# Clustered attention with a gated layer on one core: softmax factors spread from a DRAM row, and the second head's operands and masks placed by the list planner

## The chip, the cores and the metric

The kernel runs on one core of a Trainium2 chip. The metric is the device time of one execution in microseconds (us). Before the change it is 609.67 us, the median of 3 runs (608.6 to 610.37). The core has a tensor engine for matrix products (PE, whose weight loads are shown apart as PEld), a vector engine (DVE), a scalar engine (ACT), a general engine (POOL), and a sync engine (SP) that here issues every DMA. Each engine works through its own instructions in the order in which they were written; semaphores hold an instruction until what it reads is ready.

## The reference

Attention for 32 heads (4 batches of 8), in which a query sees only the keys whose nearest centroid is the same as its own, and behind it a layer that multiplies a projection with a gate from a short convolution, and projects again.

```python
def _attn_ref(q, k, v, centroids):            # q, k, v (4, 8, 768, 64), centroids (8, 16, 64)
    ...
    q_assign = np.argmax(np.einsum('bhsd,hcd->bhsc', q_n, c_n), axis=-1)
    k_assign = np.argmax(np.einsum('bhsd,hcd->bhsc', k_n, c_n), axis=-1)
    mask = q_assign[:, :, :, None] == k_assign[:, :, None, :]
    scores = scale * np.matmul(q, k.transpose(0, 1, 3, 2))
    scores = np.where(mask, scores, -1000000000.0)
    scores = scores - np.max(scores, axis=-1, keepdims=True)
    attn = np.exp(scores)
    attn = attn / (np.sum(attn, axis=-1, keepdims=True) + 1e-09)
    return np.matmul(attn, v).astype(np.float32)

def _moe_ref(x, w_val, conv_w, w_out):        # x (4, 768, 512) is the attention's output, heads side by side
    ...
    for k in range(K):                        # K = 5 taps along the sequence
        gate_pre += conv_w[k][None, None, :] * xp[:, k:k + S, :]
    gate = 1.0 / (1.0 + np.exp(-gate_pre))
    val = x @ w_val
    return (gate * val @ w_out).astype(np.float32)
```

## The kernel before

**Tiling.** A head has 768 queries in 6 tiles of 128, so there are 192 tiles; a tile is called a slot, in the order in which the tiles are computed. Heads go in 16 pairs. The first 12 slots take the heads 0 and 1 in alternation: three tiles of head 0, three of head 1, then the other three of each. Per tile, `qk` forms 128 by 768 scores in PSUM as two sums of matmuls (L410 and L415): q and k are split into a rounded high part and a remainder, called x2 and x1 for q (`prep_x2`, `prep_x1`), y1 and y2 for k (`prep_y1`, `prep_y2`), and the cluster masks are extra rows written into the operands x2 and y2 (`prep_mask0` for the first pair, `prep_mask` by DMA for the others), so that the mask comes out of the same matmul. Then DVE takes the row maximum (`rowmax`, L422), ACT the exponential with its row sum (`expo`, L431), PE transposes the tile in two groups of three blocks (L486), ACT copies these out of PSUM (`evict`, L493), and PE multiplies with v (`av`, L504).

**Softmax factors.** A pair's half (3 tiles of each of 2 heads) ends with 6 row sums per query row. `recip` inverts them on DVE (L438, L439). They lie along the partitions, but the attention output is transposed, with channels on the partitions and queries along the row, so the factors have to be spread: `recip_row` copies the 768 numbers by two DMAs into one row of one SBUF partition (the tile rr, L457), and `recip_rows` reads that row 64 times per head into 128 partitions by two DMAs (the tile rs, L464). POOL then multiplies (`scale_x`, L523). This happens 30 times. The last pair uses PE for it (`recip_b`, `recip_t`, `recip_out`).

**What sets the order.** A planner at the end of the kernel's construction holds all work as operations (`Op`: kind, engine, assumed duration, predecessors, buffers, due slot `dl`), simulates the engines with assumed costs and writes the instructions in the order that it finds. An `Op` with two engines in its table may go to either if its kind is in `FLEX`. DMAs go by the table `DMA` (time on SP, time to landing). `SIZE` holds how many buffers a name has. The planned part starts from `free`, the times at which the engines are taken to be free at its start. Ahead of the planned part stands a start-up written out by hand at the end of the function: first loads, cluster indices of the first pair, the operands of head 0, and before the change also those of head 1, with all but three of the first pair's mask copies. 94 matmuls without use (`warm`) keep PE busy in it.

**What waits on SP.** SP issues DMAs strictly in order, about 0.5 us each, so a DMA whose source isn't ready holds every one behind it.

Of the kernel before, what the change touches and what calls it, by code (L numbers as in the profile page):

```python
# [8 lines left out]
F32 = mybir.dt.float32  # L9
# [4 lines left out]
AF = mybir.ActivationFunctionType  # L14
# [3 lines left out]
P = 128  # L18
# [7 lines left out]
def kernel(  # L26
# [314 lines left out]

    def prep_x1_first(h, c0, c1):

        if ops[h][0] is None:
            ops[h][0] = operand(h, 0)
        t = gate[:, 2 + h, c0:c1]
        G.tensor_scalar(t, raws["q", h][:, c0:c1], QS, 0.0, op0=ALU.mult, op1=ALU.add)
        G.tensor_tensor(ops[h][0][:, c0:c1], t, ops[h][1][:, c0:c1].bitcast(F32), op=ALU.subtract)
# [27 lines left out]
    def prep_mask0(h, i, hf):  # L376


        n = C * (h + 1)
        dst, r = ops[h][1 + 2 * i][D:D + n, hf * HALF:(hf + 1) * HALF], 64 * hf + 32 * i  # L380
        src = oh[r:r + n, 0:HALF]
        if i == 0 and h == 0:
            S.activation(dst, src, AF.Copy)
        elif i == 0:
            G.tensor_scalar(dst, src, 1.0, 0.0, op0=ALU.mult, op1=ALU.add)
        elif h == 0:
            V.tensor_scalar(dst, src, BIG, -BIG, op0=ALU.mult, op1=ALU.add)
        else:
            S.activation(dst, src, AF.Identity, bias=oh_b1[r:r + n], scale=oh_s1[r:r + n])
# [61 lines left out]
    def recip_row(p, hf):  # L451

        sm = sums[p, hf]
        rr = sums[p, hf] = ring(am_p, 1, [P, 2, HALF], F32, "rr")[0:1]
        with nc.allow_non_contiguous_dma(reason="768 elements"):
            for e in range(2):
                nc.sync.dma_start(out=rr[:, e].rearrange("o (q t) -> o q t", t=TPH), in_=sm[:, e])  # L457

    def recip_rows(p, hf):

        rr = sums[p, hf]
        rs = ring(am_p, 1, [P, HALF], F32, "rs")
        for e in range(2):
            nc.sync.dma_start(out=rs[e * D:(e + 1) * D], in_=rr[:, e].unsqueeze(1).broadcast_to([1, D, HALF]))  # L464
# [8 lines left out]

    def recip_out(p, hf):
        acc = sums[p, hf]
        rs = sums[p, hf] = ring(am_p, 1, [P, 2, HALF], F32, "rr")[:, 0]
        S.activation(rs, acc[:, 0:HALF], AF.Copy)

    tps = {}
# [60 lines left out]
    def sigm(t, c0, c1):  # L540
# [6 lines left out]
    BURST, MBURST = 4, 4  # L547
    TOL = {"V": 0.2, "A": 0.15, "G": 2.0}
    DECODE = [24, 29, 34, 39, 52, 57, 62, 67]
    T1X = 5.0  # L550


    FLEX = ("X2", "Y1", "W1", "W3")
    CLASH = 0.8


    DMA = {"LQ": (1.15, 4.5), "LK": (1.15, 4.5), "LS": (0.42, 4.8), "LV": (0.42, 4.8), "RR": (1.2, 3.2), "RS": (1.1, 8.0),
           "MK": (1.0, 4.2), "W0": (0.6, 8.5), "ST": (0.45, 3.5)}

    hs, macc = {}, {}  # L560
# [41 lines left out]
    def proj_store(b, ch, t):  # L602
# [113 lines left out]

# [56 lines left out]
    for p in range(NPAIR):  # L773
        for hf in range(2):
# [303 lines left out]
```

## Time and profile before

| | before |
|---|---|
| median of 3 runs | 609.67 us |
| the profiled execution | 609.94 us |
| its span, first to last instruction | 608.2 us |
| DVE busy | 429.7 us (71%) |
| ACT busy | 428.3 us (70%) |
| POOL busy | 286.3 us (47%) |
| granted PE clock, mean | 0.992 |
| HBM read and written | 48.29 and 6.29 MB |

The span is 1.7 us shorter than the profiled execution; the rest lies around it. Busy times are of instructions on the engine. Times inside the trace count from the span's start. In the view by stages a row has a stretch of the span, its length, then the busy time and the number of instructions of PE, PEld, DVE, ACT and POOL, then the granted PE clock (1.00 is full speed), the mean busy share of the 16 DMA engines and the rate that they moved. In a timeline a row has start, duration, engine, line, operation, what is written <- what is read, the number of instructions, and in brackets the idle time before it with what ended it.

### The profile page before, as it was taken

Reading aid. Unit: us, or ns where it says so; the run is one execution under the profiler, and the core shown is the slowest. Engines: PE = TensorE matmul, PEld = TensorE weight load, DVE = VectorE, ACT = ScalarE, POOL = GpSimd, SP = SyncE. Lnnn points to the kernel's source line nnn. Section 1 sums busy time; section 2 is a strip of 40 time slices with the busy share of each in tenths; the row PEclk is TensorE's granted clock in tenths of the full one; section 3 lists DMA queues with packets and bytes.
Section 4 is the critical chain, followed back from the end, with each engine's and each line's share of the span. In section 5 each row is a group of like instructions: output and inputs, shape, how many; then the busy total and the mean of one; then the engine's idle time right before and its main releaser. Section 6 shows DMA issues by size and latency. Waiting matters only on the chain.

```text
span 608.2 us, 10379 instructions
## 1 busy us (share of the span) xinstructions
PE 581.2 (96%) x3592; PEld 436.3 (72%) x3592; DVE 429.7 (71%) x591; ACT 428.3 (70%) x924; POOL 286.3 (47%) x302
## 2 busy tenths in 40 slices
PE   6788899999999998999999999999999999999997
PEld 5655656566878775777786777778687777877786
DVE  5896998889889574779685476965977656863420
ACT  4856968788767775787876767777787777786321
POOL 5531767256442465294641344613653325562521
PEclk9897999999999999999999999999999999999999
DMA  8677586876787646766665667655668676431011
GB/s 246 165 115 162 125 109 121 136 113 90 133 133 101 120 54 165 136 95 96 80 128 131 90 116 125 100 62 143 76 135 134 89 133 71 21 13 38 17 53 52
DMA packets 42197, 64.21 MB, mean 106 GB/s; under 512 B 14752, under 2 KB 26912, under 8 KB 42144
## 3 DMA queue, kind: packets, MB, share of 16 engines
q1 hardware_dynamic: 42144, 63.55, 61.6%
q8 instruction: 28, 0.46, 0.3%
q14 instruction: 25, 0.20, 0.1%
HBM read 48.29 MB, written 6.29 MB: 90 GB/s over the span
## 4 chain that ended last, share of the span: by engine, by line
PE 73%; DVE 8%; DMA 7%; SPq 4%; ACT 4%; issue 2%; POOL 2%; ACTq 0%; DVEq 0%; POOLq 0%
PE acc L504 17%; PE tp L486 17%; PE sp L410 9%; PE sp L415 8%; PE acc L569 7%; PE acc L594 6%; DMA sraw<-kT 3%; PE sp L594 3%; PE sp L569 3%; DVE gate L538 3%; DVE nm L422 3%; SPq L285 2%; PE acc L290 2%; ACT pr L431 2%; DMA raw<-kT 1%
## 5 line engine op out<-in xcount | busy, mean ns | idle before, releaser
L422 DVE TENSOR_REDUCE nm<-sp 128x1 f32<-128x768 f32 x192 | 181.6, 952 | 102.2 <-PE sp L415 92.2
L493 ACT ACTIVATE pt<-tp 128x384 f32<-128x384 f32 x384 | 175.8, 492 | 76.8 <-PE tp L486 75.9
L431 ACT ACTIVATE pr<-sp,nm 128x768 f32<-128x768 f32 x192 | 173.5, 904 | 36.0 <-DVE nm L422 29.2
L486 PEld LDWEIGHTS tp<-ident,pr 128*128 128x128 f32 x1152 | 133.8, 141 | 60.1 <-issue 18.7
L486 PE MATMUL tp<-ident,pr 128*128 128x128 f32 x1152 | 168.7, 278 | 8.5 <-ACT pt L493 5.9
L504 PE MATMUL acc<-pt,vt 128*64 128x384 f32 x768 | 136.6, 495 | 0.2 <-ACT pt L493 0.2
L410 PE MATMUL sp<-op,op 128*128 128x384 f32 x372 | 111.9, 382 | 5.7 <-ACT pr L431 5.2
L538 DVE SCALAR_TENSOR_TENSOR gate<-xr,cw,gate 128x768 f32<-128x768 f32 (+1 forms) x84 | 84.1, 1006 | 18.7 <-POOL gate L86 17.9
L415 PE MATMUL sp<-op,op 80*128 80x384 f32 (+1 forms) x372 | 96.3, 340 | 0.0
L504 PEld LDWEIGHTS acc<-pt,vt 128*64 128x64 f32 x768 | 50.4, 137 | 62.1 <-issue 59.1
L523 POOL TENSOR_TENSOR xr<-xr,rs 128x384 f32<-128x384 f32 x30 | 34.9, 1163 | 112.7 <-ACT xr L516 81.1
L362 POOL TENSOR_TENSOR op<-raw,op 128x384 fp32r<-128x384 f32 x62 | 72.2, 1181 | 11.6 <-ACT op L84 10.8
L415 PEld LDWEIGHTS sp<-op,op 80*128 80x128 f32 (+1 forms) x372 | 68.4, 191 | 0.0
L410 PEld LDWEIGHTS sp<-op,op 128*128 128x128 f32 x372 | 57.1, 193 | 11.1 <-ACT pr L431 8.6
L86 POOL TENSOR_SCALAR op<-raw,qsc 128x768 fp32r<-128x768 f32 x25 | 24.2, 969 | 83.6 <-PE sp L415 77.9
L585 POOL TENSOR_TENSOR h<-gate,h 128x384 fp32r<-128x384 f32 x32 | 35.5, 1117 | 40.5 <-ACT h L581 40.5
L594 PE MATMUL acc<-wh_o,h 128*128 128x512 f32 x144 | 48.9, 399 | 0.0
L340 DVE SCALAR_TENSOR_TENSOR op<-raw,op 128x768 fp32r<-128x768 f32 x30 | 38.7, 1291 | 0.3 <-POOL op L86 0.2
L431 ACT ACTIVATION_READ_ACCUMULATOR pr<-sp,nm 128x1 f32 x192 | 38.8, 202 | 0.0
L530 POOL TENSOR_TENSOR xl<-xr,xh 128x768 fp32r<-128x768 f32 (+1 forms) x21 | 33.1, 1579 | 0.6
L569 PE MATMUL acc<-xh,wh_v 128*128 128x384 f32 x96 | 33.3, 347 | 0.0
L569 PE MATMUL acc<-xh,wl_v 128*128 128x384 f32 x96 | 32.3, 337 | 0.0
(133 smaller groups left out, 635.9 us busy)
## 6 DMA issues: line engine op xcount, KB each, us to landing
raw<-qT SPq DMA_DIRECT2D x62, 192.0 KB, 3.3
raw<-kT SPq DMA_DIRECT2D x62, 192.0 KB, 5.4
sraw<-qT SPq DMA_DIRECT2D x32, 192.0 KB, 4.9
sraw<-kT SPq DMA_DIRECT2D x32, 192.0 KB, 5.1
vt<-v SPq DMA_DIRECT2D x16, 384.0 KB, 4.2
out_dram<-ob SPq DMA_DIRECT2D x24, 256.0 KB, 2.4
rs<-rr SPq DMA_DIRECT2D x60, 96.0 KB, 7.6
op<-oht SPq DMA_DIRECT2D x56, 48.0 KB, 4.6
```

Source lines behind the costliest of these rows:

```text
L340: V.scalar_tensor_tensor(x1[:, c0:c1], raws["q", h][:, c0:c1], QS, x2[:, c0:c1], op0=ALU.mult, op1=ALU.subtract)
L362: G.tensor_tensor(y2[:, c], raws["k", h][:, c], ops[h][2][:, c].bitcast(F32), op=ALU.subtract)
L410: PE.matmul(sp[:, hf, 0:HALF], x1[:, ts_], y1[:, hf * HALF:(hf + 1) * HALF], start=True, stop=False)
L415: PE.matmul(sp[:, hf, 0:HALF], x2[0:KR, ts_], y2[0:KR, hf * HALF:(hf + 1) * HALF], start=False, stop=True)
L422: V.tensor_reduce(out=nm, in_=sp[:, :, 0:HALF], op=ALU.max, axis=AX.XY, negate=True)
L431: S.activation(pr.rearrange("p (a b) -> p a b", a=2), sp[:, :, 0:HALF], AF.Exp, bias=nm, scale=1.0, accum_out=sums[h // 2, hf][:, h % 2, t ...
L486: PE.transpose(tp[:, i * P:(i + 1) * P], pr[:, j * P:(j + 1) * P], ident)
L493: S.activation(o, tps.pop((h, t, g))[:, 0:HALF].rearrange("p (a b) -> p a b", b=P), AF.Copy)
L504: PE.matmul(acc[e * D:(e + 1) * D, 0:HALF], vt[:, j, e * D:(e + 1) * D], pts[2 * p + e, hf][:, j, :], start=(j == 0), stop=(j == NT - 1),)
L538: V.scalar_tensor_tensor(g, xr[:, k + c0:k + c1], cw[:, ct, k:k + 1], g, op0=ALU.mult, op1=ALU.add)
L569: PE.matmul(macc[b, ch, m][:, 0:HALF], a[:, kt, ms], x[:, kt, cs], start=(kt == 0 and i == 0), stop=(kt == NC - 1 and i == 2))
L594: PE.matmul(macc[b, ch, t][:, 0:DM], x[:, kt, ts_], a[:, kt, :], start=(kt == 0 and i == 0), stop=(kt == NC - 1 and i == 2))
```

## The change

1. `recip_row` writes the 768 factors with one DMA into a tile rr in DRAM (2 rows of 384, two such tiles), in place of two DMAs into a row of one SBUF partition. `recip_rows` spreads them from there, again with two DMAs. The planner's costs follow: RR takes SP 0.7 instead of 1.2, RS lands after 4.8 instead of 8.0, rr has two buffers. `recip_out` of the last pair takes the tile rs instead of rr.
2. The operands of head 1 (x2, x1, y1, y2) and its two mask copies into x2 leave the hand-written start-up and become operations of the planner, as its two mask copies into y2 already were. x2 and y1 may go to POOL or ACT; x1 comes in two halves that may go to POOL (two instructions) or DVE (one); one mask copy of head 0 may go to POOL or ACT. Three mask copies of head 0 stay written out, two of them on ACT and one on DVE, where both copies of `prep_mask0(0, 1, ...)` were on DVE.
3. `free` and the assumed arrival of head 1's q and k (`T1Q`, `T1K`) are set anew. As the planner starts from other times and other costs, the order of nearly the whole list comes out different.

```diff
+    dr_p = ctx.enter_context(tc.tile_pool(name="dr_p", bufs=1, space=bass.MemoryType.DRAM))
...
     def prep_x1_first(h, c0, c1):
 
+        if on[0] == "V":
+            prep_x1(h, c0, c1)
+            return
         if ops[h][0] is None:
             ops[h][0] = operand(h, 0)
         t = gate[:, 2 + h, c0:c1]
...
         n = C * (h + 1)
         dst, r = ops[h][1 + 2 * i][D:D + n, hf * HALF:(hf + 1) * HALF], 64 * hf + 32 * i
         src = oh[r:r + n, 0:HALF]
-        if i == 0 and h == 0:
+        if i == 0 and on[0] == "A":
             S.activation(dst, src, AF.Copy)
         elif i == 0:
             G.tensor_scalar(dst, src, 1.0, 0.0, op0=ALU.mult, op1=ALU.add)
-        elif h == 0:
+        elif h == 0 and on[0] == "V":
             V.tensor_scalar(dst, src, BIG, -BIG, op0=ALU.mult, op1=ALU.add)
         else:
-            S.activation(dst, src, AF.Identity, bias=oh_b1[r:r + n], scale=oh_s1[r:r + n])
+            x, b = (oh_s, oh_b) if h == 0 else (oh_s1, oh_b1)
+            S.activation(dst, src, AF.Identity, bias=b[r:r + n], scale=x[r:r + n])
...
     def recip_row(p, hf):
 
         sm = sums[p, hf]
-        rr = sums[p, hf] = ring(am_p, 1, [P, 2, HALF], F32, "rr")[0:1]
+        rr = sums[p, hf] = ring(dr_p, 2, [2, HALF], F32, "rr")
         with nc.allow_non_contiguous_dma(reason="768 elements"):
-            for e in range(2):
-                nc.sync.dma_start(out=rr[:, e].rearrange("o (q t) -> o q t", t=TPH), in_=sm[:, e])
+            nc.sync.dma_start(out=rr.rearrange("e (q t) -> q e t", t=TPH), in_=sm)
...
     def recip_rows(p, hf):
 
         rr = sums[p, hf]
         rs = ring(am_p, 1, [P, HALF], F32, "rs")
         for e in range(2):
-            nc.sync.dma_start(out=rs[e * D:(e + 1) * D], in_=rr[:, e].unsqueeze(1).broadcast_to([1, D, HALF]))
+            nc.sync.dma_start(out=rs[e * D:(e + 1) * D], in_=rr[e:e + 1].broadcast_to([D, HALF]))
         sums[p, hf] = rs.rearrange("p (q t) -> p t q", t=TPH)
...
     def recip_out(p, hf):
         acc = sums[p, hf]
-        rs = sums[p, hf] = ring(am_p, 1, [P, 2, HALF], F32, "rr")[:, 0]
+        rs = sums[p, hf] = ring(am_p, 1, [P, HALF], F32, "rs")
         S.activation(rs, acc[:, 0:HALF], AF.Copy)
...
-    T1X = 5.0
-
-
-    FLEX = ("X2", "Y1", "W1", "W3")
+    T1Q, T1K = -1.7, -0.2
...
-    DMA = {"LQ": (1.15, 4.5), "LK": (1.15, 4.5), "LS": (0.42, 4.8), "LV": (0.42, 4.8), "RR": (1.2, 3.2), "RS": (1.1, 8.0),
+    DMA = {"LQ": (1.15, 4.5), "LK": (1.15, 4.5), "LS": (0.42, 4.8), "LV": (0.42, 4.8), "RR": (0.7, 3.2), "RS": (1.1, 4.8),
            "MK": (1.0, 4.2), "W0": (0.6, 8.5), "ST": (0.45, 3.5)}
...
-    SIZE = {"sp": 2, "tp": 2, "pr": 3, "pt": 5, "acc": 2, "raw": 3, "sraw": 4, "vt": 2, "rr": 1, "rs": 1,
+    SIZE = {"sp": 2, "tp": 2, "pr": 3, "pt": 5, "acc": 2, "raw": 3, "sraw": 4, "vt": 2, "rr": 2, "rs": 1,
...
-    mk1 = [Op("M0", "A", 0.42, prep_mask0, 1, 1, hf, dl=1) for hf in range(2)]
-    x10 = Op("X1", "V", 0.5, prep_x1, 0, HALF, SQ, dl=3)
-    mk0 = Op("M0", "A", 0.42, prep_mask0, 0, 0, 1, after=[x10], dl=4)
-    x1_1 = done_at(T1X)
-    QK[slot[1, 0]].after += mk1 + [x1_1]
+    LQ1, LK1 = done_at(T1Q), done_at(T1K)
+    X2 = Op("X2", {"G": 0.88, "A": 0.83}, 0, prep_x2, 1, after=[LQ1], dl=2)
+    Y1 = Op("Y1", {"G": 0.81, "A": 0.74}, 0, prep_y1, 1, after=[LK1], dl=2)
+    X1 = [Op("XF", {"G": 1.75, "V": 0.5}, 0, prep_x1_first, 1, hf * HALF, (hf + 1) * HALF, after=[X2], dl=2 + 5 * hf) for hf in range(2)]
+    Y2 = [Op("Y2", "G", 0.97, prep_y2, 1, hf, after=[Y1], dl=2) for hf in range(2)]
+    x10 = Op("X1", "V", 0.5, prep_x1, 0, HALF, SQ, dl=4)
+    mk0 = Op("MQ", {"G": 0.6, "A": 0.42}, 0, prep_mask0, 0, 0, 1, after=[x10], dl=4)
+    mq1 = [Op("MQ", {"G": 0.6}, 0, prep_mask0, 1, 0, hf, after=[X2], dl=2 + 5 * hf) for hf in range(2)]
+    mk1 = [Op("MK1", "A", 0.6, prep_mask0, 1, 1, hf, after=[Y2[hf]], dl=2) for hf in range(2)]
+    QK[slot[1, 0]].after += [mq1[0], X1[0]] + mk1
+    QK[slot[1, TPH]].after += [mq1[1], X1[1]]
     QK[slot[0, TPH]].after += [x10, mk0]
...
-                RS = Op("RO", "A", 0.375, recip_out, p, hf, after=[RT], take="rr", dl=-1).frees(RT)
...
-    free = {"P": 0.0, "V": -0.4, "A": 0.0, "G": T1X, "S": 0.5}
+    free = {"P": 0.0, "V": -0.6, "A": -0.4, "G": -0.1, "S": 0.0}
...
     prep_x2(0)
+    on[0] = "G"
     prep_x1_first(0, 0, HALF)
+    on[0] = "A"
     prep_y1(0)
...
     for t in range(2):
         qk(0, t, True)
     warm(WARM[3])
-    prep_x2(1)
-    prep_y1(1)
-    prep_y2(1, 0)
-    prep_y2(1, 1)
-    prep_x1_first(1, 0, SQ)
-    prep_mask0(0, 0, 0)
-    for hf in range(2):
-        prep_mask0(0, 1, hf)
-    for hf in range(2):
-        prep_mask0(1, 0, hf)
+    for i, hf, e in ((0, 0, "A"), (1, 0, "V"), (1, 1, "A")):
+        on[0] = e
+        prep_mask0(0, i, hf)
     for o in order:
         got[0], on[0] = o.got, o.on
         o.f(*o.a)
```

In the planner's words XF is a half of head 1's x1, MQ a mask copy into x2, MK1 one into y2. Line numbers grow by 1 to 5 in this part of the changed kernel (L422 becomes L427, L431 becomes L436).

On SP, the place is from the load of head 3's q (raw) to the load of head 4's q, about 18 to 42 us in the trace of before; sraw are the inputs of a cluster group, op<-oht the mask rows of head 2, sm the inverted row sums. Before:

```order
L267 DMA vt_485<-v 128x768
L262 DMA raw_489<-qT 64x768 x2
L457 DMA rr_510<-sm_361 1x128x3 x2
L285 DMA sraw_524<-qT 128x384
L285 DMA sraw_526<-kT 128x384
L285 DMA sraw_528<-qT 128x384
L285 DMA sraw_530<-kT 128x384
L374 DMA op_1_418<-oht 16x384 x2
L374 DMA op_1_508<-oht 16x384 x2
L464 DMA rs_572<-rr_510 64x1x384 x2
L262 DMA raw_586<-kT 64x768 x2
L262 DMA raw_649<-qT 64x768 x2
```

After:

```order
L263 DMA raw_467<-qT 64x768 x2
L268 DMA vt_495<-v 128x768
L286 DMA sraw_501<-qT 128x384
L286 DMA sraw_503<-kT 128x384
L286 DMA sraw_505<-qT 128x384
L286 DMA sraw_507<-kT 128x384
L378 DMA op_1_407<-oht 16x384 x2
L378 DMA op_1_488<-oht 16x384 x2
L461 DMA rr_549<-sm_358 128x2x3
L263 DMA raw_557<-kT 64x768 x2
L468 DMA rs_582<-rr_549 64x384 x2
L263 DMA raw_625<-qT 64x768 x2
```

The copy of the factors (rr), which waits for the sums of six tiles, moves from ahead of the four sraw loads and the mask rows to behind them; the load of head 3's k moves from behind the spreading (rs) to ahead of it.

On ACT, the place is the start-up from the operands of head 0 (xh) to the second exponential; op_0 are operands of head 1, pr a tile of probabilities. Before:

```order
L84 ACTIVATE xh<-gate,qsc 128x768
L84 ACTIVATE xh<-gate 128x768
L84 ACTIVATE op_0_326<-raw_163,qsc 128x768
L84 ACTIVATE op_0_328<-raw_166 128x768
L383 ACTIVATE xh<-oh 16x384
L389 ACTIVATE op_0_330<-oh,oh_b_123,oh_s_122 32x384 x2
L383 ACTIVATE xh<-oh 16x384
L431 ACTIVATE pr_362,sm_361<-sp_279,nm_351 128x768
L431 ACTIVATE pr_369,sm_361<-sp_282,nm_359 128x768
```

After:

```order
L85 ACTIVATE xh<-gate,qsc 128x768
L85 ACTIVATE xh<-gate 128x768
L387 ACTIVATE xh<-oh 16x384
L394 ACTIVATE xh<-oh,oh_b,oh_s 16x384
L85 ACTIVATE op_0_335<-raw_168 128x768
L387 ACTIVATE xh<-oh 16x384
L436 ACTIVATE pr_359,sm_358<-sp_281,nm_348 128x768
L394 ACTIVATE op_0_354<-oh,oh_b_125,oh_s_124 32x384
L436 ACTIVATE pr_376,sm_358<-sp_284,nm_356 128x768
L497 ACTIVATE pt_389<-tp_365 128x3x128
L394 ACTIVATE op_0_354<-oh,oh_b_125,oh_s_124 32x384
```

Head 0's mask copies now stand ahead of head 1's y1, head 1's x2 is gone from ACT, and head 1's two mask copies stand behind the first and the second exponential instead of ahead of both.

On POOL, the place is the same stretch, from head 0's y2 to head 2's x2; the copies xh are head 0's, op_0 head 1's, op_1 head 2's. Before:

```order
L362 TENSOR_TENSOR xh<-gate,xh 128x384 x2
L362 TENSOR_TENSOR op_0_330<-raw_166,op_0_328 128x384 x2
L347 TENSOR_SCALAR gate<-raw_163 128x768
L348 TENSOR_TENSOR op_0_333<-gate,op_0_326 128x768
L385 TENSOR_SCALAR op_0_326<-oh 32x384 x2
L86 TENSOR_SCALAR op_1_418<-raw_348,qsc 128x768
```

After:

```order
L366 TENSOR_TENSOR xh<-gate,xh 128x384 x2
L87 TENSOR_SCALAR op_0_333<-raw_165,qsc 128x768
L366 TENSOR_TENSOR op_0_354<-raw_168,op_0_335 128x384 x2
L389 TENSOR_SCALAR op_0_333<-oh 32x384 x2
L87 TENSOR_SCALAR op_1_407<-raw_338,qsc 128x768
```

POOL takes head 1's x2 and loses its x1 (two instructions), which goes to DVE as two halves between the second and the third row maximum.

More of the change, by code (lines that the diff above doesn't have):

```diff
@@ L549 @@
     DECODE = [24, 29, 34, 39, 52, 57, 62, 67]
-    T1X = 5.0
-    FLEX = ("X2", "Y1", "W1", "W3")
+    T1Q, T1K = -1.7, -0.2
+    FLEX = ("X2", "Y1", "W1", "W3", "XF", "MQ")
     CLASH = 0.8
-    DMA = {"LQ": (1.15, 4.5), "LK": (1.15, 4.5), "LS": (0.42, 4.8), "LV": (0.42, 4.8), "RR": (1.2, 3.2), "RS": (1.1, 8.0),
+    DMA = {"LQ": (1.15, 4.5), "LK": (1.15, 4.5), "LS": (0.42, 4.8), "LV": (0.42, 4.8), "RR": (0.7, 3.2), "RS": (1.1, 4.8),
            "MK": (1.0, 4.2), "W0": (0.6, 8.5), "ST": (0.45, 3.5)}
@@ L704, in ring_started @@
             gens[name].append((len(gens[name]) % SIZE[name], o))
-    mk1 = [Op("M0", "A", 0.42, prep_mask0, 1, 1, hf, dl=1) for hf in range(2)]
-    x10 = Op("X1", "V", 0.5, prep_x1, 0, HALF, SQ, dl=3)
-    mk0 = Op("M0", "A", 0.42, prep_mask0, 0, 0, 1, after=[x10], dl=4)
-    x1_1 = done_at(T1X)
-    QK[slot[1, 0]].after += mk1 + [x1_1]
-    QK[slot[0, TPH]].after += [x10, mk0]
-    ring_started("raw", [x1_1, done_at(0.0)])
+    LQ1, LK1 = done_at(T1Q), done_at(T1K)
[9 more added lines that the diff above has]
+    QK[slot[1, TPH]].after += [mq1[1], X1[1]]
+    QK[slot[0, TPH]].after += [x10, mk0]
+    for o in X1:
+        o.users = []
+    last = done_at(0.0)
+    last.users = X1
+    ring_started("raw", [done_at(0.0)])
+    gens["raw"] += [(0, last)]
+    gens["raw"] = [(0, last)]
+    last = done_at(0.0)
+    last.users = Y2
+    gens["raw"] += [(1, last)]
+    mk1 = mk1 + mq1
     ring_started("sraw", [done_at(0.0)] * 4)
@@ L793 @@
                 late.append(RT)
-                RS = Op("RO", "A", 0.375, recip_out, p, hf, after=[RT], take="rr", dl=-1).frees(RT)
+                RS = Op("RO", "A", 0.375, recip_out, p, hf, after=[RT], take="rs", dl=-1).frees(RT)
             SX[p, hf] = Op("SX", "G", 1.1, scale_x, p, hf, after=[AVO[p, hf], RS], dl=-1).frees(RS)
```

## The prediction

> **What bounds the kernel now.** I read the page's totals first, then a view by stages, then the chain of work that ended last, and then the waits of single engines. The page:
>
> ```profile
> span 608.2 us, 10379 instructions
> PE 581.2 (96%) x3592; PEld 436.3 (72%) x3592; DVE 429.7 (71%) x591; ACT 428.3 (70%) x924; POOL 286.3 (47%) x302
> q1 hardware_dynamic: 42144, 63.55, 61.6%
> ```
>
> PE is busy for 581.2 of 608.2 us, so the tensor engine bounds the kernel, and only its 27.0 us of idle time and the time in which it runs at a lower clock are to be had. The change takes no matmul away. So the question is where these 27 us lie. The view by stages:
>
> ```profile
> 10.00:26.00 16.00, 12.34 (x93) 9.94 (x93) 12.39 (x19) 11.48 (x23) 11.67 (x13) 0.89 0.94 257
> 26.00:41.00 15.00, 14.39 (x94) 9.85 (x95) 13.90 (x28) 11.37 (x26) 4.30 (x5) 1.00 0.50 72
> 41.00:47.40 6.40, 1.59 (x10) 1.10 (x8) 5.18 (x8) 2.63 (x6) 2.51 (x3) 0.91 0.94 183
> 47.40:53.00 5.60, 5.58 (x18) 3.99 (x20) 1.99 (x3) 3.97 (x9) 1.62 (x2) 0.50 0.96 266
> 53.00:60.00 7.00, 7.00 (x50) 3.87 (x46) 5.59 (x12) 4.07 (x9) 0.00 (x0) 1.00 0.59 70
> 60.00:80.00 20.00, 17.40 (x106) 12.57 (x103) 19.27 (x27) 16.57 (x37) 15.46 (x14) 1.00 0.62 101
> 110.00:200.00 90.00, 88.81 (x559) 64.70 (x560) 79.56 (x116) 67.48 (x149) 41.79 (x39) 1.00 0.76 115
> 230.00:250.00 20.00, 17.64 (x99) 12.49 (x100) 10.86 (x17) 11.44 (x26) 9.41 (x10) 1.00 0.76 165
> ```
>
> Three places stand out. In the start-up (10 to 26) PE idles 16.00 - 12.34 = 3.7 us, and its clock is 0.89, worth 16 x 0.11 = 1.8 us. From 41.0 to 47.4 it idles 6.40 - 1.59 = 4.8 us, and then it runs at half clock for 5.6 us, which costs 2.8 us: 7.6 us for one stall. From 230 to 250 it idles 2.4 us. From 110 to 200 it idles 1.2 us in 90, so in the bulk there is little to win. DVE is the second limit early on: 13.90 of 15 us (26 to 41) and 19.27 of 20 us (60 to 80).
>
> **The change: the stall at 41 us.** The chain of work that ended last shows what led up to it; ahead of it stand SP's long wait and the three waits that make the stall (engine and line, what it waited for, us in total, times, longest):
>
> ```profile
> SPq L457 <- DVE sm L439: 9.3, 1, 9.3
> ...
> PE sp L410 <- ACT pr L431: 2.1, 1, 2.1
> PE tp L486 <- ACT pt L493: 2.7, 1, 2.7
> ...
> ACT op L84 <- DMA raw<-kT: 2.5, 1, 2.5
> ```
>
> ```profile
> 31.19 0.38 SPq L285
> 32.14 0.38 SPq L285
> ...
> 35.16 0.58 SPq L464
> 35.79 1.53 SPq L464
> 37.36 0.60 SPq L262
> 38.01 8.06 DMA raw<-kT
> ```
>
> SP stands 9.3 us at the copy of the factors, which needs the sums of six tiles. Behind it wait the four sraw loads, the mask rows, the spreading, and only then, at 37.36, the load of head 3's k. This lands at 38.01 + 8.06 = 46.07. ACT has the copy y1 of that load in its list, waits 2.5 us at it, and the eviction behind it, which PE needs, waits too. The time to landing, from the page's last part:
>
> ```profile
> raw<-qT SPq DMA_DIRECT2D x62, 192.0 KB, 3.3
> raw<-kT SPq DMA_DIRECT2D x62, 192.0 KB, 5.4
> ...
> out_dram<-ob SPq DMA_DIRECT2D x24, 256.0 KB, 2.4
> rs<-rr SPq DMA_DIRECT2D x60, 96.0 KB, 7.6
> ...
> rr<-sm SPq DMA_DIRECT2D x60, 1.5 KB, 2.0
> ```
>
> The loads of q and of k are of one size, but k's, which follow a spreading in the list, land 2.1 us later. A spreading of 96 KB takes 7.6 us where a load of 192 KB takes 3.3, so it is the reading of one SBUF partition by 64 rows that is slow, and it holds what is queued behind it.
>
> After the change three things happen to this place. The sraw loads (31.19 and its neighbours: three starts from 31.19 to 32.14, so 0.48 us each and 1.9 us for four) stand ahead of the copy, whose wait then holds them no longer. The spreading (35.16 to 37.32: 2.2 us) stands behind the load of k. And the copy is one DMA, not two, worth another 0.5 us, about the time of an issue in these rows (0.38 to 0.60). So k's load is issued at about 37.4 - 1.9 - 2.2 - 0.5 = 32.8, with no spreading ahead, and lands in 3.3 to 5.4 us, at 36 to 38, where ACT asks for it at 46.14 - 2.5 = 43.6. Its slack is over 5 us. This takes away the 2.7 us and most of the half clock behind it (2.8). The 2.1 us just ahead, where PE waits for ACT and this for DVE's row maximum, I leave as they are, and 0.5 us of the clock with them: **-5.0 us**. What is late next is DVE, which in 41 to 60 has 5.18 + 1.99 + 5.59 = 12.8 us of work in 19.0, room enough for a gain of 5. Bounds: -7.6 (the whole stall) and 0 (DVE or an eviction takes its place).
>
> **The spreading itself.** No row shows 64 reads of one DRAM row. It is bounded by 3.3 us (a load from DRAM with twice the bytes) and 7.6 us (as now); I take 3.3, since the source is what changes and the loads read DRAM. The trace doesn't show the copy of 12-byte pieces into DRAM either: below stands 2.0 us (the same pieces into SBUF), above 7.6 (the slowest of these rows); I take 2.4, a write to DRAM. Up to 7.6 it delays only what stands behind the spreading, the load of head 4's q, which is needed a head later; k's load goes out meanwhile. [...]
>
> The gain in the bulk is small because PE has no idle time there. It is the sraw loads, which wait behind spreadings. PE's waits from 200 to 300:
>
> ```profile
> PE acc L290 <- DMA sraw<-qT: 2.3, 1, 2.3
> ```
>
> That is the idle time of 230 to 250. Of these 2.3 us I take 1.5, as the list is in a new order: **-1.5 us** (bounds -2.3 and +2, a hiccup of the same size elsewhere). Thirty DMA issues fewer on SP cost or save nothing, as SP idles.
>
> **The start-up.** From the timeline:
>
> ```profile
> 10.45 2.17 POOL L362 TENSOR_TENSOR xh<-gate,xh 128x384 fp32r<-128x384 f32 x2
> 12.66 0.84 ACT L84 ACTIVATE op<-raw 128x768 fp32r<-128x768 f32 x1 [0.60 <-DMA raw<-kT]
> 13.53 0.52 ACT L383 ACTIVATE xh<-oh 16x384 fp32r<-16x384 bf16 x1
> 14.10 0.96 PE L415 MATMUL sp<-xh 80*128 80x384 f32 x4 [0.39 <-ACT xh L383]
> 14.75 1.82 DVE L422 TENSOR_REDUCE nm<-sp 128x1 f32<-128x768 f32 x2 [0.94 <-PE sp L415]
> 15.68 0.70 ACT L389 ACTIVATE op<-oh,oh_b,oh_s 32x384 fp32r<-32x384 bf16 x1 [0.27 <-POOL op L362]
> 16.53 1.81 POOL L348 TENSOR_TENSOR op<-gate,op 128x768 fp32r<-128x768 f32 x1
> 16.95 0.90 ACT L431 ACTIVATE pr<-sp,nm 128x768 f32<-128x768 f32 x1
> 20.92 0.99 PE L410 MATMUL sp<-op,op 128*128 128x384 f32 x2
> ```
>
> and from the page:
>
> ```profile
> L493 ACT ACTIVATE pt<-tp 128x384 f32<-128x384 f32 x384 | 175.8, 492 | 76.8 <-PE tp L486 75.9
> ```
>
> Head 0's closing matmuls start at 14.10, behind a mask copy that waited in ACT's list for head 1's k. After: that copy goes first, and the last one needed follows head 0's y2, done at 10.45 + 2.17 = 12.6, and takes 0.70 as L389 does: 13.35, or 0.75 us earlier. The first exponential is free of the two copies for head 1 that wait for POOL: the row maximum ends at 14.75 - 0.75 + 0.91 = 14.9, so it starts at 15.0 instead of 16.95. Head 1's first tile is then held by the second mask copy of its y2, which stands on ACT behind two exponentials (0.9 each), a first copy (0.7) and an eviction (0.5): 15.0 + 0.9 + 0.7 + 0.9 + 0.5 + 0.7 = 18.7. So it starts 2.2 us earlier than at 20.92. But DVE takes head 1's x1, two instructions of 0.5 us, and gives up a mask copy of 0.7; and it is busy for 13.90 of the next 15 us, so some of the 2.2 is lost on it: **-1.5 us** (bounds -2.2 and 0).
>
> **Sum.** -5.0 - 1.5 - 1.5 = -8.0 us from the profiled execution's 609.94 gives 601.9; that execution stands 0.3 above the median of the runs, so I say **602.0**.
>
> **The rivals.**
>
> *DVE becomes the bound.* For: its 13.90 of 15 us, and one pair of rows on line 202, alone and while POOL reads SBUF:
>
> ```profile
> L202 DVE SCALAR_TENSOR_TENSOR xl<-xl 128x512 f32<-128x512 uint32 x2 | 1.4, 682 | 0.0
> L202 DVE SCALAR_TENSOR_TENSOR h<-h 128x512 f32<-128x512 uint32 x1 | 1.8, 1785 | 0.0
> ```
>
> The same shape takes 0.68 us or 1.79. The new list places a block of eight weight-decoding instructions between the row maxima of the 9th and the 10th slot; two or three of them stretched by 1.1 us make a stall of 2 to 3 us, with half clock behind it (2.8), in place of the old one. Then the stall's -5.0 is all but lost, and -1.5 to -3 remain: about 607.5. Against: PE has 8 products with v and a cluster product to do meanwhile. [...]
>
> *The spreading isn't faster from DRAM* (slower than before). If not the source but the 64 rows or 16 engines reading the same 1.5 KB are slow, the spreading still takes 7.6 us, while the new list was planned for 4.8. Then POOL meets `scale_x` 2.8 us too early, with the next head's y2 behind it; the point from which that decides is a head whose y2 has less than 2.8 us to spare, as in the crowded part up to 110 us. Two such heads cost 2 x (2.8 + 2.8 for the clock) = 11 us; with the start-up's -1.5 and half of the stall (-5.0 / 2) this gives 610 + 7 = 617, with one such head 611.5. Against: loads from DRAM land in 3.3 us.
>
> *Everything is hidden*: the stall moves by some slots and the clock drops once more; 608 to 611.5.
>
> *More is won*: the whole stall, the sraw waits and some of the 2.6 us that PE idles from 60 to 80: -7.6 - 2.2 - 2.3 - 2 = -14, so 596.
>
> **How the numbers follow.** My forecast (597 to 605.5) gets 0.55, more won 0.09, DVE as the bound (605.5 to 608) 0.15, all hidden 0.12, slower 0.09. 0.3% is 1.8 us, about what a measurement of this kernel can tell from no change. Faster by more than that: 0.55 + 0.09 + 0.14 = 0.78; within: 0.13; slower: 0.09. The range takes in the forecast, the DVE case and part of the hidden one below, and part of the larger gain above: 595.5 to 609.5.
>
> **What would show it.** Spreadings landing in 3 to 5 us and the DMA share of q1 falling from 61.6% to about 40% (two spreadings run together, so 30 x (7.6 - 3.3) = 129 us of 608, 21 points) show the second part right; k's loads landing as fast as q's, the same. The load of head 3's k issued before 34 us and no wait of ACT for it show the stall's term; a clock of 0.5 anywhere between 40 and 60 us shows it wrong. A first exponential near 15.0 us and head 1's first matmul near 19 show the start-up. DVE above 95% from 26 to 45 us with PE waiting for row maxima would show the first rival; POOL waiting for rs in `scale_x`, the second.

## The result and the profile after

The changed kernel takes **593.73 us** (median of 4 runs, 592.86 to 594.32). The kernel before takes 609.13 us beside it (4 runs, 607.78 to 610.37). The ratio is 0.9746, with a 95% interval of 0.9719 to 0.9774: 2.5% faster, or 15.4 us. The prediction was 602.0 with a range from 595.5 to 609.5: the sign was right, but the time lies 1.8 us below the range, and the gain is nearly twice what was forecast. The profiled execution took 594.30 us, 592.5 of them span.

The page of the kernel after, its totals and the queue of the transfers:

```profile
span 592.5 us, 10305 instructions
...
PE 572.9 (97%) x3592; PEld 432.8 (73%) x3592; DVE 435.2 (73%) x589; ACT 429.3 (72%) x926; POOL 287.2 (48%) x302
...
q1 hardware_dynamic: 41664, 63.54, 43.4%
```

The same 3592 matmuls take 8.3 us less of *busy* time (572.9 against 581.2), and PE's idle time falls from 27.0 to 19.6 us. The clock explains up to 4.6 us of the first number (the 1.8 and 2.8 us of half clock that the prediction read in before are gone). That busy time falls by more than that, with no matmul taken away, is the first sign that the reading of before was incomplete.

The stages of the kernel after, in the windows shown of before (stretch, its length, PE busy, weight loads, DVE, ACT, POOL, then the granted clock, the DMA share, GB/s):

```profile
10.00:26.00 16.00, 11.52 (x98) 9.04 (x99) 15.42 (x21) 12.76 (x26) 10.02 (x12) 1.00 0.92 246
26.00:41.00 15.00, 14.32 (x96) 9.95 (x94) 13.58 (x33) 12.11 (x28) 2.54 (x4) 1.00 0.71 167
41.00:47.40 6.40, 5.98 (x40) 3.26 (x38) 5.91 (x9) 4.55 (x11) 6.40 (x5) 1.00 0.46 132
47.40:53.00 5.60, 5.60 (x40) 3.82 (x37) 5.06 (x10) 4.46 (x10) 0.02 (x1) 1.00 0.43 98
60.00:80.00 20.00, 19.00 (x119) 13.12 (x120) 19.78 (x26) 16.03 (x37) 13.23 (x13) 1.00 0.54 107
110.00:200.00 90.00, 89.26 (x576) 67.78 (x574) 79.07 (x114) 71.50 (x156) 45.16 (x42) 1.00 0.50 116
230.00:250.00 20.00, 20.00 (x119) 15.10 (x119) 11.90 (x16) 14.99 (x33) 7.00 (x7) 1.00 0.40 110
```

The stall at 41 us is gone: 5.98 of 6.40 us busy instead of 1.59, and the clock stays at 1.00 where it was 0.50. From 230 to 250 PE no longer idles (20.00, before 17.64). From 110 to 200 the busy time is almost as before (89.26, before 88.81): this view shows no gain there. Further on the windows hold other pieces of the work than before, since the kernel runs ahead, so such a view can't say where the rest was won; that takes kernels with one order.

The last part of the page (median time from issue to landing), and SP's issues at the place of the old stall:

```profile
raw<-qT SPq DMA_DIRECT2D x62, 192.0 KB, 4.7
raw<-kT SPq DMA_DIRECT2D x62, 192.0 KB, 3.7
...
rs<-rr SPq DMA_DIRECT2D x60, 96.0 KB, 3.1
...
rr<-sm SPq DMA_DIRECT2D x30, 3.0 KB, 3.8
```

```profile
30.53 0.53 SPq L461 DMA_DIRECT2D rr<-sm  x1
31.11 1.15 SPq L263 DMA_DIRECT2D raw<-kT  x2
34.63 1.09 SPq L468 DMA_DIRECT2D rs<-rr  x2
```

A spreading lands in 3.1 us instead of 7.6, the copy takes 3.8 (one DMA of 3.0 KB) instead of 2.0 (each of two of 1.5 KB), and head 3's k goes out at 31.11.

### The profile page after: what moved, and what is told of

Read it like the earlier page. It is cut to its first block, busy times and chain, and to the rows that moved or that the text cites. A ratio compares the mean times of both kernels' runs of the same rounds, so it can differ in the third digit from the quotient of the medians.

```text
span 592.5 us, 10305 instructions
## 1 busy us (share of the span) xinstructions
PE 572.9 (97%) x3592; PEld 432.8 (73%) x3592; DVE 435.2 (73%) x589; ACT 429.3 (72%) x926; POOL 287.2 (48%) x302
## 3 DMA queue, kind: packets, MB, share of 16 engines
q1 hardware_dynamic: 41664, 63.54, 43.4%
## 4 chain that ended last, share of the span: by engine, by line
PE 71%; DVE 11%; ACT 5%; issue 5%; POOL 4%; DMA 2%; SPq 1%; ACTq 0%; POOLq 0%; DVEq 0%
PE acc L508 17%; PE tp L490 17%; PE sp L415 9%; PE sp L420 8%; PE acc L573 7%; PE acc L598 6%; DVE nm L427 4%; DVE gate L542 4%; ACT pr L436 3%; PE sp L598 2%; PE sp L573 2%; PE acc L291 2%; POOL h L589 1%; DMA raw<-qT 1%; ACT pt L497 1%
## 5 line engine op out<-in xcount | busy, mean ns | idle before, releaser
L427 DVE TENSOR_REDUCE nm<-sp 128x1 f32<-128x768 f32 x192 | 181.3, 952 | 88.0 <-PE sp L420 73.9
L436 ACT ACTIVATE pr<-sp,nm 128x768 f32<-128x768 f32 x192 | 173.2, 903 | 33.9 <-DVE nm L427 26.8
L490 PE MATMUL tp<-ident,pr 128*128 128x128 f32 x1152 | 167.0, 276 | 6.2 <-ACT pt L497 3.0
L542 DVE SCALAR_TENSOR_TENSOR gate<-xr,cw,gate 128x768 f32<-128x768 f32 (+1 forms) x84 | 92.4, 1105 | 13.4 <-POOL gate L87 12.6
L527 POOL TENSOR_TENSOR xr<-xr,rs 128x384 f32<-128x384 f32 x32 | 37.8, 1180 | 110.4 <-ACT xr L520 83.8
L341 DVE SCALAR_TENSOR_TENSOR op<-raw,op 128x768 fp32r<-128x768 f32 (+1 forms) x32 | 40.2, 1257 | 0.2
L436 ACT ACTIVATION_READ_ACCUMULATOR pr<-sp,nm 128x1 f32 x192 | 38.7, 201 | 0.0
L573 PE MATMUL acc<-xl,wh_v 128*128 128x384 f32 x96 | 32.3, 337 | 0.0
```

Of the source, the lines that this page charges most:

```text
L427: V.tensor_reduce(out=nm, in_=sp[:, :, 0:HALF], op=ALU.max, axis=AX.XY, negate=True)
L436: S.activation(pr.rearrange("p (a b) -> p a b", a=2), sp[:, :, 0:HALF], AF.Exp, bias=nm, scale=1.0, accum_out=sums[h // 2, hf][:, h % 2, t ...
L490: PE.transpose(tp[:, i * P:(i + 1) * P], pr[:, j * P:(j + 1) * P], ident)
L542: V.scalar_tensor_tensor(g, xr[:, k + c0:k + c1], cw[:, ct, k:k + 1], g, op0=ALU.mult, op1=ALU.add)
L573: PE.matmul(macc[b, ch, m][:, 0:HALF], a[:, kt, ms], x[:, kt, cs], start=(kt == 0 and i == 0), stop=(kt == NC - 1 and i == 2))
```

## The experiments

Twelve kernels were run, with 3 or 5 rounds of timing each. Differences are taken between medians of one comparison; the interval is that of the ratio. Kernels of different comparisons are set against each other by what each wins over its own before (15.4 us for the changed kernel).

| run | order | row of factors | us | before | ratio [95%] | spreading lands |
|---|---|---|---|---|---|---|
| e1 | before | DRAM | 598.33 | 609.54 | 0.9785 [0.9732, 0.9839] | 3.1 |
| e2 | replanned, start-up of before | DRAM | 597.01 | 609.54 | 0.9783 [0.9740, 0.9825] | 3.0 |
| e3 | replanned, start-up of after | SBUF | 608.33 | 609.54 | 0.9968 [0.9947, 0.9988] | 7.3 |
| e4 | after | SBUF | 621.60 | 609.54 | 1.0182 [1.0143, 1.0222] | 8.2 |
| e5 | before | SBUF, partitions 0 and 64 | 600.32 | 609.43 | 0.9856 [0.9815, 0.9897] | 5.6 |
| e6 | before | first of 30 in DRAM | 604.51 | 609.43 | 0.9927 [0.9898, 0.9955] | 7.6 |
| e7 | before | other 29 in DRAM | 600.54 | 609.43 | 0.9844 [0.9797, 0.9892] | 2.9 |
| e8 | planned with measured costs | DRAM | 601.73 | 609.43 | 0.9877 [0.9833, 0.9920] | 3.2 |
| e9 | before | twelfth of 30 in DRAM | 604.00 | 609.95 | 0.9909 [0.9881, 0.9937] | 7.6 |
| e10 | before, one k load moved | SBUF | 606.56 | 609.95 | 0.9956 [0.9932, 0.9979] | 6.9 |
| e11 | after | SBUF, partitions 0 and 64 | 595.88 | 609.95 | 0.9777 [0.9743, 0.9811] | 5.5 |
| e12 | before | SBUF, partitions 0 and 1 | 608.95 | 609.39 | 0.9997 [0.9964, 1.0030] | 7.7 |

### The parts of the change apart (e1 to e4)

Theory A: the fast spreading gives the gain. Theory B: the new order gives it.

**e1** puts the row into DRAM and leaves the order of every engine as it was:

```diff
...
-        rr = sums[p, hf] = ring(am_p, 1, [P, 2, HALF], F32, "rr")[0:1]
+        rr = sums[p, hf] = ring(dr_p, 2, [2, HALF], F32, "rr")
...
-            for e in range(2):
-                nc.sync.dma_start(out=rr[:, e].rearrange("o (q t) -> o q t", t=TPH), in_=sm[:, e])
+            nc.sync.dma_start(out=rr.rearrange("e (q t) -> q e t", t=TPH), in_=sm)
...
```

> The row of factors lies in DRAM (one copy, spread from there), and the planner's numbers are left as they were before, so that every engine has the order of before and SP only one copy less per half pair. Theory A (what counts is that spreadings from one SBUF partition no longer hold the DMA engines and SP): 598 to 602 us, spreadings landing in about 3 us, no wait of ACT for head 3's k near 44 us and no wait of PE for cluster inputs near 232 us, as these two stalls have 7.6 and 4 to 5 us in the trace of before. Theory B (what counts is the new order of the list): 606 to 609 us, with the stall near 44 us moved but not gone.

598.33 us: A. From 41 to 47.4 us PE is busy for 4.22 us instead of 1.59 and the clock stays at 1.00, and from 230 to 250 PE is busy throughout. **e2** adds the planner's new costs to it (copy 0.7 on SP, spreading 4.8, two rows), with the start-up of before.

> The whole first part of the change (row in DRAM with the planner's new costs), with the start-up of before. Theory A: 596 to 600 us, a little under the run with the old order, since the planner now knows the shorter times. Theory B: 603 to 608 us, since the start-up and the planner's start times are those of before.

597.01 us: A; the new costs add 1.3 us, less than these runs can tell from nothing. **e3** is the reverse: the changed kernel's start-up and start times, the row in SBUF and the old costs.

> The second and third part of the change alone (head 1's operands and masks in the list, new start times), with the row in SBUF and the old costs. Theory A: 604 to 608 us: the start-up gives at most the 1 to 2 us by which the first exponential and head 1's first matmul came earlier in the changed kernel, and the stalls behind spreadings stay. Theory B: 595 to 600 us.

608.33 us, 0.3 over A's range: the start-up alone is worth 1.2 us. On top of the DRAM row it is worth 2.9 (e2 wins 12.5, the changed kernel 15.4). **e4** takes the changed kernel's order on every engine and puts the row back into SBUF.

> The changed kernel's order on every engine, with the row in one SBUF partition again (two copies and slow spreadings). Theory A: 602 to 607 us, with spreadings of about 7.6 us and PE waiting for cluster inputs or for operands at several places. Theory B: 594 to 597 us, as the order alone carries the gain.

621.60 us: both theories missed. An order planned for spreadings that land in 4.8 us, with spreadings of 8.2, is 12.1 us slower than before, and 27.5 slower than the same order with the DRAM row. With slow spreadings the order earns nothing; with the DRAM row, the new order and the new start-up together win 4.2 us on top of e1's 11.2.

### Which spreadings pay (e6, e7, e9)

The prediction gave 5.0 us to the stall at 41 us and 1.5 to all the rest. With the order of before, e6 sends only the first row (the one ahead of head 3's k) through DRAM, and e7 (with `!=`) all but the first:

```diff
+        if (p, hf) == (0, 0):
+            rr = sums[p, hf] = ring(dr_p, 2, [2, HALF], F32, "rd")
+            nc.sync.dma_start(out=rr.rearrange("e (q t) -> q e t", t=TPH), in_=sm)
+            return
...
```

> The kernel of before, order untouched; only the first of the 30 rows of factors (the one whose spreading stands ahead of head 3's k, at 35 us) goes through DRAM, the other 29 through SBUF. Theory S (as predicted: the stall at 41 us is worth 5.0, the bulk 1.5): 603.5 to 606. Theory T (the bulk's 29 spreadings are worth most, some 8 us, and the stall 3 to 5): 604.5 to 607. The two differ in the run with the other 29.

> The reverse: the first row of factors through SBUF as before, the other 29 through DRAM, order untouched. Theory S (the bulk is worth 1.5): 606.5 to 608.5. Theory T (the bulk is worth some 8 us): 600 to 603, with 4 to 5 us of it near 230 us.

e6: 604.51, 4.9 us won. e7: 600.54, 8.9 us won. Theory T. Since PE runs the same matmuls in the same order in both, matmul n of one can be set against matmul n of the other. For e7 the lead over before grows by 1.6 us at 122 us of before's time, by 1.2 at 169, by 4.6 at 234, by 1.4 at 329, by 1.2 at 397 and by 0.5 at 471. Each place is a cluster product (L290 of before), or stands right behind one. e1 wins 11.2 us, less than the 13.8 of e6 and e7 together. The difference lies in the start: at 40 us e1's trace is 2.1 us behind before's (its clock is 0.79 from 10 to 26), and from there it wins 4.9 at the stall and 8.7 behind it. The groups of the cluster products, in before and in e7 (busy us, mean ns | idle ahead of it):

```profile
L290 PE MATMUL acc<-sraw,cenT 128*32 128x384 f32 x128 | 21.3, 497 | 4.0 <-DMA sraw<-qT 2.7 <-DMA sraw<-kT 1.0 <-DVE cenT L151 0.3
```

```profile
L291 PE MATMUL acc<-sraw,cenT 128*32 128x384 f32 x128 | 15.1, 498 | 0.1
```

128 matmuls of the same mean length, yet 21.3 us of busy time against 15.1. With the idle time ahead of them, 25.3 against 15.2 us: 10.1 us, which is the whole gain of e7 (its lead at the end is 9.7). Not all of it is the row's doing. e12 (below) keeps its rows in SBUF and takes as long as before, and its group stands between the two:

```profile
L290 PE MATMUL acc<-sraw,cenT 128*32 128x384 f32 x128 | 20.7, 516 | 3.0 <-DMA sraw<-qT 2.8 <-PE tp L395 0.2
```

That is 23.7 us, 8.5 more than e7. Steps of 1.0 to 1.1 us against before at 169 and 329 stand in e12 and in e6 as well, whose spreadings there are the slow ones, so those two come and go between executions; the ones at 122, 234 and 397, 7.4 us together, are won in full only where the spreading is faster. The product near 326, in before and in e12 (start, length, what ran, how many):

```profile
325.85 1.11 PE L290 MATMUL acc<-sraw,cenT 128*32 128x384 f32 x6
327.27 0.83 PE L290 MATMUL acc<-sraw,cenT 128*32 128x384 f32 x2 [0.31 <-DMA sraw<-kT]
```

```profile
325.74 1.27 PE L290 MATMUL acc<-sraw,cenT 128*32 128x384 f32 x8
```

The timeline shows how a wait comes to stand under busy time. Four lines of before, then one of e9:

```profile
119.67 2.35 PE L290 MATMUL acc<-sraw,cenT 128*32 128x384 f32 x8 [0.41 <-DMA sraw<-qT]
...
183.21 0.85 PE L290 MATMUL acc<-sraw,cenT 128*32 128x384 f32 x8
...
231.88 1.86 PE L290 MATMUL acc<-sraw,cenT 128*32 128x384 f32 x6 [2.25 <-DMA sraw<-qT]
234.22 0.83 PE L290 MATMUL acc<-sraw,cenT 128*32 128x384 f32 x2 [0.49 <-DMA sraw<-kT]
```

```profile
229.37 0.86 PE L291 MATMUL acc<-sraw,cenT 128*32 128x384 f32 x8
```

With all four operands there, as at 183.21, the spans of the eight matmuls lie over one another, and they take 0.85 us together. When the operands land one after another, the matmuls start one after another, and the union of their spans counts as busy: 2.35 us at 119.67, 1.5 more than without waiting. Near 232 the product ends at 234.22 + 0.83 = 235.05; ahead of it PE is idle for 2.25 us, so it costs 5.4 us with the idle times, where e9 takes 0.86 and no idle time: 4.6 us.

e9 tests one place alone, the twelfth row (`(5, 1)` in the condition), whose spreading starts at 222.27.

> The kernel of before, order untouched; only the twelfth of the 30 rows of factors (pair 5, second half, whose spreading starts at 222.27 us ahead of four sraw loads) goes through DRAM. Theory T (this one spreading holds SP and the loads behind it, and PE loses 4.2 us there): 604.5 to 606.5, PE busy for all of 230 to 250. Theory U (what was won at that place with all rows in DRAM came from the calmer DMA queues as a whole, this spreading alone gives what PE's own waits show, 2.3 or less): 607 to 609.5.

604.00 us: 6.0 won, half a microsecond more than T allowed. The lead grows by 4.6 us at this place, and by 1.4 more near 329 us, where the spreadings are as before; that second step is the one that also comes and goes in e6 and e12. SP's issues in before, and then in e9 (start, length):

```profile
222.27 1.13 SPq L464 DMA_DIRECT2D rs<-rr  x2
223.45 0.73 SPq L285 DMA_DIRECT2D sraw<-qT  x1
224.23 3.64 SPq L285 DMA_DIRECT2D sraw<-kT  x1
227.91 0.43 SPq L285 DMA_DIRECT2D sraw<-qT  x1
```

```profile
221.98 1.09 SPq L471 DMA_DIRECT2D rs<-rd  x2
223.12 0.58 SPq L286 DMA_DIRECT2D sraw<-qT  x1
223.75 0.43 SPq L286 DMA_DIRECT2D sraw<-kT  x1
224.22 0.43 SPq L286 DMA_DIRECT2D sraw<-qT  x1
```

Behind two slow spreadings, SP spends 3.64 us on the issue of one load where 0.43 is usual, and the two loads behind it go out 3.7 us late. The transfers of the same stretch, 216 to 236 us, in 40 slices of 0.5 us (busy share of the DMA engines in tenths, and GB/s), before and e9:

```profile
DMA  2985000000000019969969798998499999899999
GB/s 74 289 209 215 0 0 0 0 0 0 0 0 0 0 12 40 31 18 31 34 18 34 22 28 25 28 28 28 101 329 396 399 415 289 154 252 227 252 277 230
```

```profile
DMA  0332574000000013579995999999872100001016
GB/s 0 12 25 74 129 295 148 6 0 0 0 0 0 0 68 144 157 187 372 317 197 98 237 313 341 237 301 283 252 184 43 39 0 0 0 0 3 0 3 242
```

In before the DMA engines read as busy for 60% and more over 13 slices (6.5 us) and move 18 to 40 GB/s in them (28 on the mean); then up to 415. In e9 the loads run with the spreading.

### The stall by order alone (e10)

Only the two DMAs of head 3's k are moved ahead of the first spreading; the row stays in SBUF.

```diff
-    def recip_rows(p, hf):
+    def recip_rows(p, hf, now=False):
+        if (p, hf) == (0, 0) and not now:
+            late_rows.append((p, hf))
+            return
...
         raws[nm, h] = t
+        while nm == "k" and late_rows:
+            recip_rows(*late_rows.pop(), now=True)
```

> The kernel of before with one change of order: on SP the load of head 3's k (two DMAs, at 37.36) goes out ahead of the first spreading (two, at 35.16) instead of behind it; the row stays in SBUF. As predicted for the stall (k's load held by the spreading): the load lands at about 35.2 + 4 = 39, ACT doesn't wait for it, and the stall goes: 603.5 to 606. Rival (the spreading, now later, keeps POOL and the operands behind it, or the sraw loads of 43 us, just as long): 607.5 to 610.

606.56 us, 3.4 won, between the two. The spreading now stands ahead of the next load and holds that:

```profile
35.44 2.31 SPq L262 DMA_DIRECT2D raw<-kT  x2
37.80 1.24 SPq L470 DMA_DIRECT2D rs<-rr  x2
39.09 4.50 SPq L262 DMA_DIRECT2D raw<-qT  x2
```

Of the stall's 4.9 us, the place of the load gives some 3.4 without any faster spreading (by the intervals 1.3 to 4.1 here, 2.7 to 6.2 in e6); most of it came from the load that stood behind the spreading, as predicted.

### What is slow in the spreading (e5, e12, e11)

Both spreadings of a pair read partition 0. e5 puts the second head's row on partition 64; e12 has `rr[e:e + 1, e]` in the two places, which is partition 1:

```diff
-        rr = sums[p, hf] = ring(am_p, 1, [P, 2, HALF], F32, "rr")[0:1]
+        rr = sums[p, hf] = ring(am_p, 1, [P, 2, HALF], F32, "rr")
...
-                nc.sync.dma_start(out=rr[:, e].rearrange("o (q t) -> o q t", t=TPH), in_=sm[:, e])
+                nc.sync.dma_start(out=rr[e * D:e * D + 1, e].rearrange("o (q t) -> o q t", t=TPH), in_=sm[:, e])
...
-            nc.sync.dma_start(out=rs[e * D:(e + 1) * D], in_=rr[:, e].unsqueeze(1).broadcast_to([1, D, HALF]))
+            nc.sync.dma_start(out=rs[e * D:(e + 1) * D], in_=rr[e * D:e * D + 1, e].unsqueeze(1).broadcast_to([1, D, HALF]))
```

> The kernel of before with one edit: the second head's row of factors lies on partition 64 instead of partition 0, so each of the two spreadings of a pair reads a partition of its own; order and everything else as before. Theory P (the reading of one SBUF partition by both spreadings at once is what is slow): two partitions share the reads, the spreadings land in 3.8 to 4.5 us instead of 7.6, the DMA share of q1 falls from 61.6% to 45 to 50%, and the time comes near that of the DRAM row in the old order, 598 to 602. Theory Q (each spreading is slow by itself, 64 rows fetched from the same 1.5 KB of SBUF): the spreadings still land in 7 to 8 us, 607 to 611.

> As the kernel with the row on partitions 0 and 64 (5.6 us, 600.3), but on the neighbours 0 and 1, in the order of before. If it is the single partition that the two spreadings contend for: 5.4 to 5.8 us and 599 to 602, as with 0 and 64. If neighbouring partitions share what they contend for: 7.2 to 7.7 us and 607 to 611.

The landings, first of e5 and then of e12:

```profile
rs<-rr SPq DMA_DIRECT2D x60, 96.0 KB, 5.6
```

```profile
rs<-rr SPq DMA_DIRECT2D x60, 96.0 KB, 7.7
```

Partition 64 makes it 5.6 us (slower than theory P's 3.8 to 4.5) and 600.32, with a DMA share of 50.4%; partition 1 changes nothing, 608.95. So, as far as these two runs show, it isn't the single partition that the reads contend for, but something that 0 and 1 share and 0 and 64 don't. What that is, no run shows.

e11 is e4 with the row on partitions 0 and 64.

> The changed kernel's order on every engine, with the row in SBUF, the second head's on partition 64. If the new order needs only that a spreading lands in some 5 us: 594 to 600. If it needs the DRAM row's 3.1 us, since the spreadings here land 0.8 us later than planned and hold the loads behind them: 602 to 610.

595.88 us, 14.1 won: 26.1 better than e4 with 8.2 us, and 1.3 short of the DRAM row. The new order needs spreadings of some 5 us, not of 3.

### Better costs for the planner (e8)

The changed kernel's table has a copy of 3.2 us and a spreading of 4.8; its trace shows 3.8 and 3.1. e8 plans with 4.0 and 3.2.

```diff
-    DMA = {... "RR": (0.7, 3.2), "RS": (1.1, 4.8),
+    DMA = {... "RR": (0.55, 4.0), "RS": (1.1, 3.2),
```

> The changed kernel with the planner's costs set to what its trace shows: a copy into DRAM 4.0 us in all and 0.55 on SP (it has 3.2 and 0.7), a spreading 3.2 (it has 4.8). The order on every engine comes out different. If the wrong costs still cost waits: 590 to 592.5. If the rest of PE's idle time has nothing to do with the spreadings: 592.5 to 596.5, no difference.

601.73 us: a miss. It wins 7.7 us, half of what the changed kernel wins, with spreadings as fast (3.2 us). From 110 to 200 us PE is busy for 87.10 of 90 (89.26 in the changed kernel), from 200 to 230 for 28.86 of 30 (30.00), and the clock is 0.89 from 10 to 26 and 0.83 from 90 to 100 (1.00 in both). The loss lies in several small places, and which decision of the planner starts them stays open. No version ran faster than the changed kernel.

## Why the prediction was right or wrong

**The spreading: right.** 3.3 us were taken, 3.1 measured; the DMA share of q1 fell to 43.4% (forecast: about 40).

**The copy into DRAM: too cheap**, 2.4 taken and 3.8 measured, inside the bounds. The prediction argued that this changes nothing; no run isolates it. In before the copy took 2.0 us (each of two of 1.5 KB into SBUF), here 3.8 (one of 3.0 KB into DRAM); place and size differ together, and no run shows which of them makes it dearer.

**The stall: right,** -5.0 forecast and -4.9 measured (e6; its interval is -6.2 to -2.7). In e6's trace the lead over before grows by 5.1 us between 40 and 55 us. In the changed kernel the k load went out at 31.11 (forecast about 32.8), ACT doesn't wait for it, and the clock stayed at 1.00. By e10, some 3.4 of it come from the load that stood behind the spreading.

**The start-up: right within what can be told,** -1.5 forecast, -1.2 alone (e3; interval -3.2 to -0.7) and -2.9 on top of the DRAM row. In the kernel after:

```profile
15.82 0.90 ACT L436 ACTIVATE pr<-sp,nm 128x768 f32<-128x768 f32 x1
...
19.30 0.60 PE L415 MATMUL sp<-op,op 128*128 128x384 f32 x2
```

The first exponential starts at 15.82, not at 15.0; head 1's first matmul at 19.30, near the 18.7 to 19. Of the steps, the 0.75 us for head 0's closing matmuls can't be told: they start at 14.10 in before, at 13.98 here and at 15.11 in e3, which has the same start-up. From them to head 1's first matmul it is 6.8 us in before, 5.3 here and 5.1 in e3, so that part came. The clock from 10 to 26 us, 0.89 in before and 1.00 here, doesn't follow the start-up's code: it is 0.89 in e3, e4 and e8, which have the new one, and 1.00 in e2, which has the old. Whether its 1.8 us belong to the change stays open.

**The bulk: this term failed.** The step reads: "The gain in the bulk is small because PE has no idle time there. It is the sraw loads, which wait behind spreadings", and then "Of these 2.3 us I take 1.5". It measured -8.9 (e7; interval -12.4 to -6.6). The mechanism named was the right one (sraw loads behind spreadings); its size was read from PE's idle time alone. Two things went amiss. First, the argument from "only its 27.0 us of idle time ... are to be had": a product whose operands trickle in is counted busy while it waits, so 6.2 us of e7's gain (21.3 - 15.1) lay inside the busy time. The trace of before holds this: its 128 matmuls are 16 products of eight, at 0.85 us each 13.6 us, and 21.3 busy + 4.0 idle stand there, 11.7 us more. Second, the view of PE's waits was read for the one long wait of 2.3 us; the same place cost 4.6, since SP stood 3.64 us at an issue and the loads came one by one.

With the terms as measured, -4.9 - 8.9 - 1.2 = -15.0 from 609.1 gives 594.1; the result is 593.73. That it closes so well is luck in part: the first two terms were measured in the order of before. In the changed kernel the cluster products win 6.8 us (25.3 to 18.5), not 10.1, as three of the sixteen still take 1.7 to 2.7 us where 0.85 would do:

```profile
156.93 1.72 PE L291 MATMUL acc<-sraw,cenT 128*32 128x384 f32 x8
...
229.14 2.19 PE L291 MATMUL acc<-sraw,cenT 128*32 128x384 f32 x8
...
303.45 2.65 PE L291 MATMUL acc<-sraw,cenT 128*32 128x384 f32 x8 [0.22 <-DVE op L341]
```

The rest comes from elsewhere; the clock of the start-up may be part of it. In the prediction's own sum, the 0.3 us by which the profiled execution stood above the median were left in (601.7 without them), which changes nothing.

**The rivals.** *DVE as the bound* didn't come: from 26 to 45 us DVE is busy for 17.58 of 19.00 us, under the 95% that was its sign, and from 60 to 80 for 19.78 of 20, with PE still at 19.00. That POOL's reads stretch DVE's instructions was not shown by a run: in before the L202 row of 1.79 us starts at 37.55, with POOL at L236 from 37.44 to 38.78, and one of 1.03 us starts at 133.51, with POOL busy throughout. *The spreading isn't faster* fell, and its price was too low: e4 is that case, 621.6 where 611.5 to 617 was worked out. Its sign came, POOL waiting for rs in `scale_x` (26.3 us in five waits; in before 8.0 in two); but the sraw loads, which it didn't count, carry a good part. L290 in e4:

```profile
L290 PE MATMUL acc<-sraw,cenT 128*32 128x384 f32 x128 | 26.1, 533 | 4.0 <-DMA sraw<-kT 3.0 <-DMA sraw<-qT 1.1
```

That is 30.1 us of busy and idle time, where the changed kernel has

```profile
L291 PE MATMUL acc<-sraw,cenT 128*32 128x384 f32 x128 | 18.2, 498 | 0.3 <-DVE op L341 0.2
```

18.5: 11.6 of the 27.5 us. *More is won*, 596, came nearest in its number but by other terms: 7.6 for the stall, 2.2 for the start-up, 2 for the stretch from 60 to 80, and only 2.3 for the sraw waits.

## What to carry to other kernels

A tensor engine that is 96% busy can still be waiting (the cluster products: 21.3 us of busy time in before, 15.1 in e7). Compare the busy time of a group of matmuls with what the same group takes where all its operands are there, and add the difference to the idle time before saying how much can be won.

A slow transfer is paid for by whatever is queued behind it (here 4.9 us at the stall, by e6, and 8.9 at the other places, by e7). List what each one holds (loads, and the engine that issues them), all along the kernel and not only at the worst stall; and an order planned for fast transfers is a loss if they stay slow (12.1 us in e4).

## What the runs showed of the hardware

- Spreading one row over 64 channels, twice at a time: 7.6 us from SBUF partition 0 (before), 7.7 from partitions 0 and 1 (e12), 5.6 from 0 and 64 (e5), 3.1 from DRAM (after).
- Behind two spreadings from SBUF, an issue on SP took 3.64 us instead of 0.43 (224.23 in before), and over 6.5 us the DMA engines read as busy for 60% and more while they moved 18 to 40 GB/s (216 to 236 us in before).
- The eight matmuls of a cluster product, each 128*32 by 128x384, took 0.85 us together with their operands there, and 2.35 where these arrived one by one (at 183.21 and 119.67 in before).
- The loads of q, which now follow the spreadings, land in 4.7 us (after) instead of 3.3 (before); those of k in 3.7 instead of 5.4 (medians).
